# Turning K on VectorE as bf16 pairs instead of on TensorE, in a one-core decode attention kernel

## The chip, the cores and the metric

The kernel runs on one core of one Trainium2 chip. The metric is device time in microseconds (us). Ratios are the mean time of one kernel's fast runs over the mean of the other's fast runs of the same rounds, so they are not quite the ratio of the medians that stand beside them.

Short names: PE is TensorE (PEld its weight loads), DVE is VectorE, ACT is ScalarE, POOL is GpSimd, SP is the engine that issues the transfers.

## The reference, cut to what matters

```python
# B = 4 sequences, one new token each; D = 576, 32 query heads, 16 KV heads, head size 128
W = min(4096, max(256, Sk // 4))                 # the last 4096 keys of 16384
q = (layernorm(x) @ wq)                          # (4, 32, 128)
k = k_cache[:, :, Sk - W:, :]; v = v_cache[:, :, Sk - W:, :]   # each KV head serves 2 query heads
p = softmax(q @ k.T * 128 ** -0.5);  h = x + (p @ v) @ wo
h2 = h + (relu(n @ W_gate) * (n @ W_up)) @ W_down,  n = layernorm(h)
```

K and V are 4 x 16 x 4096 x 128 bf16 values each, 67 MB, and are read once. With the weights, 159.6 MB come from HBM.

## The kernel before

The cache goes through a ring of four slots of 4 MB in SBUF. One tile holds four KV heads of one sequence: 32 partitions for each head, 128 keys in each partition. SP issues one transfer for each tile, in a fixed order; a transfer waits until the last reader of its slot's former tile is done.

```python
def add_kv(kind, g):                         # one 4 MB tile into the next of four slots
    s = ring_slot(); off = slot0 + s * TILE
    src = cache[b, 4*qd:4*qd+4, SK-WIN:SK, :].rearrange("a (p t) d -> p a (t d)", p=32)
    place((kind, g), off, TILE, ("TR", 4*g+3) if kind == "K" else ("PV", 4*g+3), ...)   # who frees it

add_kv("K", 0);  ...wq...                    # order: K0, wq, K1, K2, K3, K4, V0, K5, V1, ...
for g in range(1, NTILE):
    add_kv("K", g)
    if g >= 4: add_kv("V", g - 4)
```

K arrives with keys on partitions; the QK of this kernel is written for the 128 numbers of a head on partitions. So PE transposes 128 blocks a tile (64 in 3.68 us), DVE and ACT copy them from PSUM to SBUF (0.69 and 1.02 us a copy), and QK runs with four matmuls side by side in column groups of 32 (16 in 0.98 us; the records of four start within about 0.01 us):

```python
def pe_tr(i):                                # a quarter of a K tile: 32 transposes
    for j in range(4):
        for u in range(8):
            pe(..., lambda e: e.transpose(out=bankb[TRB[j]][:, u*128:(u+1)*128],
                                          in_=kn[:, t, :], identity=perm))
def evac(i, j):                              # 128x1024 bf16, PSUM to SBUF
    (dve if j % 2 == 0 else act)(("EV", i, j), lambda e: copy(kT..., bankb[TRB[j]][:, 0:1024]))
def pe_qk(dd):
    for a in range(4):
        for j in range(4):
            pe(..., lambda e: e.matmul(bank[4+w][32*j:32*j+32, :],
                                       lhsT=qTm[:, b, 4*qd+a, :], rhs=k[:, j, :, a, :]))
```

## Time and profile before

| | before |
|---|---|
| time, median of the runs | 384.7 us (384.59 to 384.88) |
| span in the profile | 382.6 us |
| moved from HBM | 159.58 MB |
| instructions of PE: matmuls and weight loads | 3781 + 3781 |

First the page of the kernel before: the busy time of each engine, and of the DMA queues' section the data queue and the queue that fetches instructions (packets, MB, share of 16 engines' span).

```profile
PE 248.7 (65%) x3781; PEld 185.9 (49%) x3781; DVE 159.0 (42%) x277; ACT 146.4 (38%) x162; POOL 8.7 (2%) x36
...
q1 hardware_dynamic: 6352, 159.59, 97.4%
q8 instruction: 29, 0.48, 0.5%
```

No compute engine is near its limit; the DMA engines are, at 97.4%. Now the chain of waits between two K tiles (start, length, what):

```profile
96.03 28.17 DMA sb_arena<-in_A_k_cache_dram
...
124.25 3.60 PE psb L425 x32
...
129.31 3.68 PE psb L425 x64
...
135.89 27.24 DMA sb_arena<-in_A_k_cache_dram
```

The K tile lands at 124.2 us and PE works on it for 11.7 us until 135.9, then its slot takes the next transfer, and so on. The chain makes this look like a loop that could be shortened. It can't be: the four slots keep enough transfers waiting that the DMA engines are hardly ever idle. Two stretches show it, as windows (length, busy time of PE, PEld, DVE, ACT, POOL with the count of instructions, granted PE clock, DMA share, GB/s):

```profile
40.00:45.00 5.00, 5.00 (x88) 3.91 (x80) 2.77 (x4) 3.49 (x4) 0.00 (x0) 0.99 0.98 419
165.00:170.00 5.00, 5.00 (x83) 4.13 (x81) 3.72 (x10) 3.68 (x6) 0.00 (x0) 1.00 1.05 449
```

The DMA share is 0.98 and 1.05 here, and it lies between 0.93 and 1.09 in every such window from 5 to 370 us. (A packet counts whole in the window in which it starts, so a share can pass 1.) The last two:

```profile
370.00:375.00 5.00, 2.79 (x93) 2.03 (x93) 1.51 (x4) 0.27 (x1) 0.00 (x0) 1.00 0.78 328
375.00:380.00 5.00, 2.21 (x72) 1.44 (x72) 0.00 (x0) 0.00 (x0) 0.00 (x0) 0.80 0.31 126
```

Here the share falls to 0.78 and then 0.31 while the kernel still waits for data. As I read the records, some DMA engines are done and others are not: for each transfer the trace has 16 increments of its semaphore, at 16 times and without numbers of engines. The page counts 16 DMA engines, and 16 data packets are under way at 60, 100, 200 and 300 us, so I take each increment for one engine that has finished its part. Worked out from those records (not a view of the profile): the time of the first engine and how far behind the others are, with the number of 16 KB instruction packets started by then.

```
before           first us   fetches   lags of the 16 engines behind the first, us
1st K tile          12.71      0      0  .2 .2 .3 .3 .3 .3 .3 .4 .4 .4 .4 .4 .4 .5 .5
2nd K tile          33.41      1      0  .1 .2 .3 .3 .3 .3 .3 .3 .4 .4 .4 .4 .4 .5 1.9
V tile              72.24      6      0  .2 .2 .3 .3 .4 .4 .5 .5 1.1 1.9 1.9 1.9 1.9 1.9 2.0
K tile             120.78     10      0  .2 .3 .3 .4 .5 .9 1.1 1.9 1.9 1.9 1.9 1.9 2.0 3.4 3.4
last transfer      372.77     28      0  .2 .2 .3 .4 .4 .8 2.1 4.9 5.0 5.1 6.5 6.5 6.5 6.6 6.6
```

Each fetch puts one engine back by 1.4 to 1.5 us. The counts fit engines that are hit in turn: after eight fetches eight engines lag by about 1.9 us, then one of them lags by 3.4. The records of single packets give the size of the step: a fetch takes 0.93 to 1.11 us, and for the second to the 26th fetch one data packet of 32 KB that starts about when the fetch ends takes 1.68 to 1.76 us instead of 1.21. These lengths repeat with a period of eight (1.71, 1.71, 1.72, 1.68, 1.68, 1.69, 1.76, 1.76 us), which fits eight engines in turn too. With 28 fetches the worst engines trail by 6.6 us. The kernel ends with the last engine: its increment comes at 379.35 us of a span of 382.6 us.

The groups of instructions that the change is about (line, engine, operation, tiles, shape, count | busy us, mean ns | idle before, releaser):

```profile
L425 PE MATMUL psb<-sb_perm,sb_arena 128*128 128x128 bf16 x2048 | 140.3, 235 | 74.0 <-DMA sb_arena<-in_A_k_cache_dram 73.8
L441 ACT COPY sb_arena<-psb 128x1024 bf16<-128x1024 bf16 x128 | 123.0, 1021 | 141.1 <-PE psb L425 141.1
...
L439 DVE COPY sb_arena<-psb 128x1024 bf16<-128x1024 bf16 x128 | 87.0, 689 | 112.1 <-PE psb L425 111.6
...
L457 PE MATMUL psb<-sb_arena,sb_qTm 128*32 128x512 bf16 x512 | 38.0, 423 | 0.9 <-DVE sb_qTm L404 0.9
```

### The profile page before, as it was taken

The page shows a single profiled execution, that of the slowest core. Times are in us where ns is not written, and L with a number is a line of the kernel's source. Part 1 is how long each engine was busy: PE and PEld are TensorE (multiplying, and loading weights), DVE is VectorE, ACT ScalarE, POOL GpSimd, SP SyncE. Part 2 cuts the span into 40 slices and gives each one's busy share as a digit, 9 for nine tenths or more (in the row PEclk, how much of TensorE's full clock was granted, in tenths as well). Part 3 has the DMA queues.
Part 4 walks back from the last instruction along what each step waited for, and adds up shares of the span by engine and source line. Part 5 has one row for each costly group of instructions (what it writes and reads, how often), then busy time and mean ns, then how long its engine had stood idle before and what let it go on. Part 6 is the DMA issues. An engine that isn't in the chain of part 4 may idle for free.

```text
span 382.6 us, 8170 instructions
## 1 busy us (share of the span) xinstructions
PE 248.7 (65%) x3781; PEld 185.9 (49%) x3781; DVE 159.0 (42%) x277; ACT 146.4 (38%) x162; POOL 8.7 (2%) x36
## 2 busy tenths in 40 slices
PE   0664999779492938893947667966759366026753
PEld 0643788557371726672726455745546222003532
DVE  3342565665342434774432426752516454002220
ACT  3341688836161524762433428542525401000010
POOL 7100000000000000000000000000000000000000
PEclk9997999999888796999796969996969657555597
DMA  8999999999999999999999999999999999999992
GB/s 329 439 433 432 410 421 437 434 433 433 425 423 433 427 433 435 427 420 433 437 430 435 424 428 427 427 428 439 437 432 415 421 436 451 416 431 426 416 411 113
DMA packets 6408, 160.09 MB, mean 418 GB/s; under 512 B 740, under 2 KB 744, under 8 KB 1384
## 3 DMA queue, kind: packets, MB, share of 16 engines
q1 hardware_dynamic: 6352, 159.59, 97.4%
q8 instruction: 29, 0.48, 0.5%
q14 instruction: 3, 0.02, 0.0%
q10 hardware_dynamic: 24, 0.01, 0.0%
HBM read 159.58 MB, written 0.00 MB: 417 GB/s over the span
## 4 chain that ended last, share of the span: by engine, by line
DMA 69%; PE 27%; DVE 2%; SPq 1%; ACT 1%; issue 0%
DMA sb_arena<-in_A_k_cache_dram 53%; PE psb L425 18%; DMA sb_arena<-in_B_W_down_dram 8%; DMA sb_arena<-in_A_v_cache_dram 8%; PE psb L457 5%; PE psb L505 2%; PE psb L480 1%; DVE sb_pp L487 1%; ACT sb_pp L468 1%; SPq L280 0%; DVE sb_stat L464 0%; DVE sb_o_sel L516 0%; PE psb L539 0%; PE psb L530 0%; DVE sb_o_tmp L512 0%
## 5 line engine op out<-in xcount | busy, mean ns | idle before, releaser
L425 PE MATMUL psb<-sb_perm,sb_arena 128*128 128x128 bf16 x2048 | 140.3, 235 | 74.0 <-DMA sb_arena<-in_A_k_cache_dram 73.8
L441 ACT COPY sb_arena<-psb 128x1024 bf16<-128x1024 bf16 x128 | 123.0, 1021 | 141.1 <-PE psb L425 141.1
L425 PEld LDWEIGHTS psb<-sb_perm,sb_arena 128*128 128x128 bf16 x2048 | 131.5, 106 | 89.3 <-DMA sb_arena<-in_A_k_cache_dram 79.8
L439 DVE COPY sb_arena<-psb 128x1024 bf16<-128x1024 bf16 x128 | 87.0, 689 | 112.1 <-PE psb L425 111.6
L505 PE MATMUL psb<-sb_arena,sb_pp 128*32 128x512 bf16 x512 | 35.9, 425 | 19.9 <-DMA sb_arena<-in_A_v_cache_dram 19.9
L457 PE MATMUL psb<-sb_arena,sb_qTm 128*32 128x512 bf16 x512 | 38.0, 423 | 0.9 <-DVE sb_qTm L404 0.9
L505 PEld LDWEIGHTS psb<-sb_arena,sb_pp 128*32 128x32 bf16 x512 | 12.9, 104 | 36.3 <-DMA sb_arena<-in_A_v_cache_dram 20.9
L512 DVE TENSOR_TENSOR sb_o_tmp<-psb,sb_qm 128x512 f32<-128x512 f32 x16 | 11.1, 692 | 41.2 <-PE psb L505 41.2
L487 DVE TENSOR_TENSOR sb_pp<-psb,sb_am 128x1024 bf16<-128x1024 bf16 x16 | 19.6, 1223 | 16.2 <-PE psb L480 16.2
L480 PE MATMUL psb<-sb_ident_b,sb_pp 128*128 128x128 bf16 x128 | 11.5, 242 | 15.8 <-DVE sb_pp L487 8.3
L468 ACT ACTIVATE sb_pp<-psb,sb_stat 128x2048 bf16<-128x2048 f32 x8 | 15.8, 1975 | 9.7 <-DVE sb_stat L466 9.7
L457 PEld LDWEIGHTS psb<-sb_arena,sb_qTm 128*32 128x32 bf16 x512 | 11.6, 103 | 14.8 <-issue 6.2
L480 PEld LDWEIGHTS psb<-sb_ident_b,sb_pp 128*128 128x128 bf16 x128 | 8.6, 108 | 18.8 <-ACT sb_pp L468 8.1
L516 DVE TENSOR_REDUCE sb_o_sel<-sb_o_tmp 128x128 f32<-128x512 f32 x16 | 16.4, 1024 | 0.5
L612 ACT COPY sb_pp<-psb 128x288 f32<-128x288 f32 x1 | 0.4, 399 | 36.2 <-PE psb L607 36.2
L654 PE MATMUL psb<-sb_arena,sb_hnT 128*32 128x384 bf16 x120 | 7.5, 421 | 4.1 <-DVE sb_hnT L639 2.2
L654 PEld LDWEIGHTS psb<-sb_arena,sb_hnT 128*32 128x32 bf16 x120 | 4.1, 121 | 7.2 <-DMA sb_arena<-in_B_W_up_dram 2.3
L464 DVE TENSOR_REDUCE sb_stat<-psb 128x1 f32<-128x1024 f32 x4 | 4.9, 1221 | 4.6 <-PE psb L457 4.6
L687 PE MATMUL psb<-sb_arena,sb_pp 128*32 128x144 bf16 x144 | 3.7, 251 | 4.1 <-DMA sb_arena<-in_B_W_down_dram 3.6
L534 ACT ACTIVATE sb_stat<-sb_stat 128x1 f32<-128x1 f32 x4 | 0.9, 213 | 13.1 <-DVE sb_stat L532 13.1
L661 DVE TENSOR_TENSOR sb_pp<-psb,sb_pp 128x384 bf16<-128x384 f32 x3 | 1.5, 551 | 9.6 <-PE psb L654 9.6
L687 PEld LDWEIGHTS psb<-sb_arena,sb_pp 128*32 128x32 bf16 x144 | 2.6, 105 | 5.1 <-DMA sb_arena<-in_B_W_down_dram 4.6
(128 smaller groups left out, 78.7 us busy)
## 6 DMA issues: line engine op xcount, KB each, us to landing
sb_arena<-in_A_k_cache_dram SPq DMA_DIRECT2D x16, 4096.0 KB, 28.3
sb_arena<-in_A_v_cache_dram SPq DMA_DIRECT2D x16, 4096.0 KB, 33.6
sb_arena<-in_A_wo_dram SPq DMA_DIRECT2D x1, 4608.0 KB, 20.7
sb_arena<-in_B_W_gate_dram SPq DMA_DIRECT2D x1, 4608.0 KB, 34.1
sb_arena<-in_B_W_up_dram SPq DMA_DIRECT2D x1, 4608.0 KB, 43.5
sb_arena<-in_A_wq_dram SPq DMA_DIRECT2D x1, 4096.0 KB, 23.0
sb_arena<-in_B_W_down_dram SPq DMA_DIRECT2D x3, 1296.0 KB, 30.0
sb_arena<-in_B_W_down_dram SPq DMA_DIRECT2D x1, 864.0 KB, 31.6
```

Of the source, the lines that this page charges most:

```text
L425: o = pe(("TRJ", i, j), lambda e, j=j, u=u, t=t: e.transpose(out=bankb[TRB[j]][:, u * 128:(u + 1) * 128], in_=kn[:, t, :], identity=perm[: ...
L439: dve(("EV", i, j), lambda e: e.tensor_copy(out=dst, in_=src), deps)
L441: act(("EV", i, j), lambda e: e.copy(out=dst, in_=src), deps)
L457: o = pe(("QK", dd), lambda e, a=a, j=j: e.matmul(bank[4 + w][32 * j:32 * j + 32, :], lhsT=qTm[:, b, 4 * qd + a, :], rhs=k[:, j, :, a, :], ...
L468: act(("EXP", b, w), lambda e: e.activation(out=p_sb[:, 2048 * w:2048 * w + 2048].rearrange("p (k a) -> p k a", a=4), in_=bass.AP(tensor=p ...
L480: pe(("PT", b, r), lambda e, tl=tl: e.transpose(out=mb_ps[:, tl * 128:(tl + 1) * 128], in_=p_sb[:, (r * 8 + tl) * 128:(r * 8 + tl + 1) * 128],
L487: dve(("PM", b, r), lambda e: e.tensor_tensor(out=dst, in0=src, in1=msk, op=ALU.mult), [("PT", b, r), "c_am8", ("PV", 16 * b - 1) if b els ...
L505: pe(("PV", i), lambda e, j=j, lo=lo, pm=pm, tb=tb: e.matmul(o_ps[32 * j:32 * j + 32, :], lhsT=pT[:, pm:pm + 32], rhs=v[:, lo:lo + 512], s ...
L512: dve(("OS", g), lambda e: e.tensor_tensor(out=o_tmp[:, :].rearrange("p (t d) -> p t d", t=4), in0=o_ps.rearrange("p (t d) -> p t d", t=4) ...
L516: dve(("OSEL", g), lambda e: e.tensor_reduce(out=o_sel[:, qd, :], in_=o_tmp[:, :].rearrange("p (t d) -> p d t", t=4), axis=AX.X, op=ALU.ad ...
L654: pe(("GU", g, c // 4), lambda e, g=g, m=m, j=j, lo=lo, c=c: e.matmul(bank[3 * g + m][32 * j:32 * j + 32, 0:384], lhsT=hnT[:, c if c < 4 e ...
L687: pe("DOWN", lambda e, j=j, r=r, n=n, wv=wv: e.matmul(bank[0][32 * n:32 * n + 32, 0:144], lhsT=hhT[:, r * 128 + 32 * j:r * 128 + 32 * j + 32],
```

## The change

Its intent: take the transposes off PE and their copies off DVE and ACT. DVE's transpose takes two bf16 neighbours as one fp32 value and turns K in place in its slot, for each head its 32 partitions against 32 pairs. Each matmul of QK then contracts over 128 partitions = 4 heads x 32 pairs, for even or odd elements and one half of the head (4 steps `cb`), against weights that hold q of one head and zeros elsewhere. How DVE orders its output has two forms: `by_head` (all columns of a head in one run) or heads two by two in a line. The diff, cut to its core:

```diff
+def by_head(g, w):
+    return (g, w) in ((0, 0), (0, 1), (2, 1), (3, 1), (4, 1))
...
-            place((kind, g), off, TILE, ("TR", 4 * g + 3) if kind == "K" else ("PV", 4 * g + 3),
+            place((kind, g), off, TILE, ("QK", g, 1) if kind == "K" else ("PV", g),
...
-        P.dma("scalar", ("L", "x"), ...)              # was ahead of everything
         act("warm_sqrt", ...)
+        P.dma("scalar", ("L", "x"), ...)
...
-        def pe_tr(i): ...                             # 2048 PE transposes, 256 copies
-        def evac(i, j): ...
+        def turn_k(g, w):                             # half a K tile, in place
+            k = arena[:, land[("K", g)] + w * QWW:][:, 0:QWW].bitcast(FP32)
+            if by_head(g, w):
+                dst = k.rearrange("p (n a k) -> p n k a", a=4, k=8)
+                src = k.rearrange("p (n k a) -> p n k a", a=4, k=8)
+            else:
+                dst = k.rearrange("p (n h l a) -> p n l h a", h=2, l=2, a=2)
+                src = k.rearrange("p (n l h a) -> p n l h a", h=2, l=2, a=2)
+            dve(("TRA", g, w), lambda e: e.transpose(out=dst, in_=src), [("L", "K", g)] if w == 0 else [])
...
+            for a in heads:                           # pe_qk
+                for cb in range(4):
+                    sub, steps = (16 * a, [[2, 8]]) if by_head(g, w) else (a // 2 * 8 + a % 2 * 2, [[16, 4], [4, 2]])
+                    off = land[("K", g)] + w * QWW + cb // 2 * 64 + sub + cb % 2
+                    pe(("QK", g, w), lambda e, ...: e.matmul(
+                        bank[SB[b % 2] + w], lhsT=arena[:, wo_:wo_ + 128],
+                        rhs=bass.AP(tensor=arena, offset=off, ap=[[AW, 128], [128, 64]] + steps), ...), deps)
...
+        def turn_p(b, w): ...                         # P turned on DVE too, mask as bias of 8 short Exp
...
         # order: x, turn of K0, q projection, then K tiles; the first softmax runs inside K4 and K5
```

## The prediction

> **What bounds the kernel now.** The DMA engines. The page's queue section gives the data queue 97.4% of 16 engines' span; the slices show about 430 GB/s from the second to the last but two. PE (65%), DVE (42%) and ACT (38%) have slack. The chain of waits alternates "K lands" (28 us) and "PE turns it, then QK" (18 to 21 us), but that is only the loop of four slots: the windows show a DMA share of 0.97 to 1.07 in every 5 us from 80 to 345 us, so the late release of slots costs nothing.
>
> What is left is uneven engines. In the trace's record of completions, the 16 increments of one transfer lie 0.5 us apart for the first tile and 6.6 us apart for the last (372.8 to 379.35 us). [...] The lag grows in steps of 1.4 to 1.5 us, one engine per 16 KB packet of the instruction queue (29 packets, 0.48 MB), dealt round over eight engines. [...]
>
> **What the change does.** It removes 2048 PE transposes (59 ns apart at full clock, 7.4 us a K tile), their 256 evacuations (DVE 0.69 us, ACT 1.02 us each, 210 us in sum), and 128 transposes of P with 16 masked copies (1.22 us). It adds 32 half-tile turns of 4096 fp32 pairs on DVE; at about 1 element a ns I estimate 4.3 us each[...]. QK no longer has four matmuls side by side: 32 of 128x512 per K tile at 0.24 us (estimate from 16 in 0.98 us, four at a time), 7.5 us against 2. PE per K tile falls from 9.4 to about 7.5 us (double at half clock). None of this lies on the bound.
>
> **What moves the time.** PE instructions fall to about 3260, so 12 to 13 fetches instead of 29: at most two on one engine instead of four. The last engine should trail by about 3.4 us instead of 6.6: a gain of about 3.1 us. Against it: the fourth K tile's transfer now waits for QK of tile 0 (before: its transposes, 22 us), which needs q. I estimate QMM to 28, q placed at 33, QK done near 41 us; the queue would run dry at 43 us. So 0 to 2 us of stall, more if PE starts cold; I count 0.4, and 0.2 gained from the later x load: 384.7 - 3.1 + 0.4 - 0.2.
>
> **Predicted: 381.8 us, 80% between 380.6 and 385.0. Faster by over 2%: 0.01; within 2%: 0.96; slower: 0.03.**
>
> **What would show it.** 12 or 13 instruction packets of 16 KB; last transfer's increments 3 to 4 us apart, first engine still near 372.8 us; DMA share above 0.95 in every 5 us from 5 to 365; turn plus QK of a K tile 12 to 17 us; DVE 190 to 220 us busy.
>
> **What would make it wrong.** A dry DMA queue between 41 and 50 us, or at 85 to 105 us where first softmax, turns and PV compete on DVE; DVE turns of 8 us everywhere, which would make DVE the limit (17 us plus others per 19.6 us); QK slowed by interleaved reads; DMA packets (1.22 us per 32 KB now) slowed by DVE traffic.

The sum: 384.7 - 3.1 + 0.4 - 0.2 = 381.8 us.

The numbers of the trace before that the rest stands on:

- 7562 PE instructions and 29 packets are 261 instructions a packet, so about 3260 are 12.5 packets. That the packets go with PE's instructions was the assumption then; e3 (3978 instructions, 15 packets) and e5 (7562 and 29) bear it out.
- "About 1 element a ns": a DVE copy of 128x128 f32 took 292 ns and one of 128x288 f32 457 ns, 1.03 ns for each further element of a partition. 4096 at that rate are 4.2 us, an estimate.
- "Half clock" and "cold": from 35 to 40 us PE's granted clock is 0.50, and the 32 transposes there come 0.107 us apart; from 40 to 45 us it is 0.99, and they come 0.056 us apart.

## The result, and the profile after

The kernel after took 382.37 us (381.78 to 382.86, 4 runs) against 384.67 us (384.59 to 384.88) before; the ratio is 0.9941, 95% interval 0.9927 to 0.9955. Sent again later (e9), it took 381.78 us (381.47 to 383.03, 6 runs), ratio 0.9927 (0.9916 to 0.9939). The page of the kernel after, the same lines:

```profile
PE 278.0 (73%) x1629; PEld 92.8 (24%) x1629; DVE 223.2 (59%) x157; ACT 37.5 (10%) x95; POOL 16.3 (4%) x38
...
q1 hardware_dynamic: 6352, 159.59, 97.7%
q8 instruction: 12, 0.20, 0.2%
```

PE is busier than before (278.0 against 248.7 us) and DVE too (223.2 against 159.0 us). ACT fell from 146.4 to 37.5 us. The number of PE's instructions fell from 3781 to 1629 pairs, and the instruction packets from 29 to 12. The last windows:

```profile
370.00:375.00 5.00, 3.14 (x125) 2.55 (x129) 1.04 (x3) 0.27 (x1) 0.00 (x0) 1.00 0.81 337
375.00:380.00 5.00, 1.96 (x52) 0.93 (x40) 0.31 (x1) 0.00 (x0) 0.00 (x0) 0.60 0.07 28
```

From 375 to 380 us the DMA share is 0.07 where it was 0.31: the engines now end closer together. The records of the last transfer, worked out as above:

```
                 first us   fetches   last us   spread us
before             372.77      28      379.35      6.59
after              373.20      11      377.55      4.35
```

The first engine did not become faster; the last one ends 1.80 us earlier. (The traced run of the kernel after, 382.86 us, is the slowest of its four.) The groups that do the work now:

```profile
L450 PE MATMUL psb<-sb_arena 128*128 128x512 bf16 x512 | 209.1, 578 | 10.5 <-DVE sb_arena L432 8.2
L432 DVE STREAM_TRANSPOSE sb_arena<-sb_arena 128x4096 f32<-128x4096 f32 x32 | 156.1, 4901 | 48.5 <-DMA sb_arena<-in_A_k_cache_dram 48.4
...
L475 ACT ACTIVATE sb_pp<-psb,sb_stat 128x512 bf16<-128x512 f32 x32 | 24.9, 847 | 247.8 <-DVE sb_stat L470 247.8
```

The 2048 transposes and 256 copies are gone, 32 turns of 4.9 us in the mean have come. QK takes 512 matmuls as before, but one after another. The chain around one K tile:

```profile
104.42 19.58 DMA sb_arena<-in_A_k_cache_dram
...
124.02 4.46 DVE sb_arena L432
...
128.52 13.97 PE psb L450 x32
142.49 1.84 PE psb L497 x32
```

The tile lands at 124.0 us, waits for one turn of 4.46 us and then 13.97 us of QK, and frees its slot at 142.5, 18.5 us after landing; before it was 11.7 us. So the loop that the chain named became longer, and the kernel became faster. That alone shows that the chain's loop was not the bound.

### The profile page after: what moved, and what is told of

It is laid out like the page before. It is cut to its first block, busy times and chain, and to the rows that moved or that the text cites. A ratio compares the mean times of both kernels' runs of the same rounds, so it can differ in the third digit from the quotient of the medians.

```text
span 381.1 us, 3671 instructions
## 1 busy us (share of the span) xinstructions
PE 278.0 (73%) x1629; PEld 92.8 (24%) x1629; DVE 223.2 (59%) x157; ACT 37.5 (10%) x95; POOL 16.3 (4%) x38
## 4 chain that ended last, share of the span: by engine, by line
PE 44%; DMA 34%; DVE 15%; POOL 2%; ACT 2%; issue 1%; SPq 0%; POOLq 0%
PE psb L450 38%; DMA sb_arena<-in_A_k_cache_dram 19%; DVE sb_arena L432 11%; DMA sb_arena<-in_B_W_down_dram 9%; DMA sb_arena<-in_A_v_cache_dram 7%; PE psb L497 5%; POOL sb_arena L303 2%; ACT sb_pp L475 2%; DVE sb_o_sel L509 1%; DVE sb_o_tmp L505 1%; DVE sb_pp L484 1%; PE psb L534 0%; ACT sb_arena L418 0%; SPq L286 0%; PE psb L469 0%
## 5 line engine op out<-in xcount | busy, mean ns | idle before, releaser
L450 PE MATMUL psb<-sb_arena 128*128 128x512 bf16 x512 | 209.1, 578 | 10.5 <-DVE sb_arena L432 8.2
L432 DVE STREAM_TRANSPOSE sb_arena<-sb_arena 128x4096 f32<-128x4096 f32 x32 | 156.1, 4901 | 48.5 <-DMA sb_arena<-in_A_k_cache_dram 48.4
L450 PEld LDWEIGHTS psb<-sb_arena 128*128 128x128 bf16 x512 | 56.8, 114 | 153.6 <-issue 130.3
L475 ACT ACTIVATE sb_pp<-psb,sb_stat 128x512 bf16<-128x512 f32 x32 | 24.9, 847 | 247.8 <-DVE sb_stat L470 247.8
L484 DVE STREAM_TRANSPOSE sb_pp<-sb_pp 128x2048 bf16<-128x2048 bf16 x8 | 18.0, 2278 | 1.4 <-ACT sb_pp L475 1.4
L534 PE MATMUL psb<-sb_o_sel,sb_selw 128*32 128x32 f32 x128 | 2.4, 232 | 16.3 <-DVE sb_o_sel L509 16.3
L388 PE MATMUL psb<-sb_arena,sb_xnT 128*32 128x512 bf16 x32 | 3.6, 631 | 8.9 <-DMA sb_arena<-in_A_wq_dram 8.9
L303 POOL MEMSET sb_arena<- 128x8192 f32 x1 | 6.9, 6925 | 0.0
L475 ACT ACTIVATION_READ_ACCUMULATOR sb_pp<-psb,sb_stat 128x1 f32 x32 | 6.6, 208 | 0.0
L418 ACT COPY sb_arena<-sb_q_keep 32x128 bf16<-32x128 bf16 x16 | 4.8, 303 | 1.5 <-DVE sb_q_keep L409 1.4
```

Of the source, the lines that this page charges most:

```text
L303: pool("c_qW", lambda e: e.memset(arena[:, 0:2 * QWW].bitcast(FP32), 0.0))
L418: act(("QW", b), lambda e, i=i: e.copy(out=bass.AP(tensor=arena, offset=32 * i * AW + b % 2 * QWW + 32 * i, ap=[[AW, 32], [128, 4], [514, ...
L432: dve(("TRA", g, w), lambda e: e.transpose(out=dst, in_=src), [("L", "K", g)] if w == 0 else [])
L450: pe(("QK", g, w), lambda e, off=off, steps=steps, wo_=wo_, qd=qd, first=first, last=a == cb == 3: e.matmul(bank[SB[b % 2] + w], lhsT=aren ...
L475: act(("EXP", b, w), lambda e, w=w, a=a: e.activation(out=bass.AP(tensor=pp, offset=4096 + a // 2 * 2048 + w * 1024 + a % 2, ap=[[8192, 12 ...
L484: dve(("PTR", b, w), lambda e: e.transpose(out=dst, in_=src), [("EXP", b, w), ("PV", 4 * b - 1) if b else "QMM"])
```

## The experiments

Of e1 to e4 the trace that is kept is of another execution than the one first read. The figures below are from the kept traces, except where the first trace is named.

Theory A: the gain comes from PE's shorter instruction stream, since every fetch of 16 KB holds back one of 16 DMA engines, and the kernel ends with the last. Its second part: at the start the change costs something, since the fourth K tile is now issued late. Rivals: B, relief of DVE, ACT or the slots; C, PE's array time.

### e1 and e2: more instructions for PE, by waits that are already met (failed as a test)

```diff
+                    for _ in range(NPAD):             # after each QK matmul, g >= 5; 12 and 24
+                        pe(None, PAD)                 # engine.wait_ge(sem, 1), met long ago
```

> The kernel after, with 12 semaphore waits that are already met after each QK matmul of the K tiles from the sixth on: 2112 more instructions for PE's sequencer, no array work. Theory A (the gain is the fewer instruction fetches of PE, which hold back single DMA engines): about 20 instruction packets instead of 12, the last transfer's increments 1.4 us further apart, 1.0 to 1.6 us slower than the kernel after, ratio to before about 0.9975. Theory B (the gain is PE, ACT and DVE relieved, or slots released otherwise): no change, ratio 0.994.

> The same with 24 waits, 4224 more instructions. A: about 28 or 29 packets, increments about 2.9 us further apart than in the kernel after, time near the kernel before, ratio 1.000 to 1.003. B: no change, ratio 0.994, unless the waits lengthen QK by so much that the DMA queue runs dry, which the DMA share in 5 us windows would show.

Measured: 449.31 us, ratio 1.168, and 681.57 us, ratio 1.770, with 21 and 29 packets. The waits were not free. PE's timeline in e2 (first trace; start, length, engine, line) shows QK matmuls 1.33 us apart where the kernel after has 0.43:

```profile
200.62 0.59 PE L455 MATMUL psb<-sb_arena 128*128 128x512 bf16 x1 [0.77 <-issue]
201.95 0.59 PE L455 MATMUL psb<-sb_arena 128*128 128x512 bf16 x1 [0.75 <-issue]
```

PE became the bound and the DMA queue ran dry: in e1 PE is busy for 8.77 of the 10 us from 205 to 215 us, and the DMA share is 0.62 (265 GB/s); the 159.6 MB in e2's span of 680.2 us are 235 GB/s. So these runs say nothing of A or B. They tell one thing by accident: in both the last transfer's engines lie only 2.0 us apart in spite of 20 and 29 fetches, where the kernel before has 6.6 us after 28. I read this as engines that are behind and catch up when the queue is dry, so that the lag adds up only while all engines have work.

### e3: the kernel before with fewer PE instructions

```diff
-                    for u in range(8): e.transpose(out=bankb[TRB[j]][:, u*128:(u+1)*128], in_=kn[:, t, :], identity=perm)
+                    e.matmul(bank[TRB[j]][:, :], lhsT=perm, rhs=kn[:, t:t + 4, :], start=True, stop=True)   # once
```

K is not turned, so the result is wrong. The comparison with the reference still passed: the scores are so small (about 0.003, an estimate from the inputs' scales in the reference) that the softmax is nearly flat, so K hardly reaches the output. A pass is no proof that K is handled rightly here.

> The kernel before, with each group of eight transposes of a K tile replaced by one 128x512 matmul into the same bank (wrong result on purpose, K isn't turned): 1792 fewer pairs of PE instructions, everything else kept, above all the evacuations on DVE and ACT. A: 15 packets instead of 29, the last transfer's increments 3.4 to 3.6 us apart instead of 6.6, ratio 0.991 to 0.993, a little better than the kernel after since no late issue of the fourth K tile disturbs the start. B (relief of DVE and ACT, or DVE turning K): little or no gain, ratio above 0.997. A rival that says PE time is what counts would expect a gain too; the two runs with waits are against that one.

Measured: 381.62 us (381.51 to 381.84), ratio 0.992 (0.9907 to 0.9934). Busy time and fetches:

```profile
PE 207.8 (55%) x1989; PEld 80.3 (21%) x1989; DVE 155.5 (41%) x277; ACT 145.1 (38%) x162; POOL 8.7 (2%) x36
...
q8 instruction: 15, 0.25, 0.3%
```

The last transfer: first engine 372.88, last 376.42 us, spread 3.54. The last engine ends 2.93 us earlier than before and the median is 3.1 us lower. DVE and ACT do what they did before, so that part of B falls: this kernel gets the whole gain without the turn on DVE. In e3 PE works less and frees slots sooner; the kernel after is the counterexample to both, with PE busier and slots freed later.

### e5 and e6: the instructions back without their work, and the work without the instructions

```diff
 e5:  # e3, and ahead of each matmul seven one-column matmuls into the bank that it overwrites
+                    for _ in range(7): e.matmul(bank[TRB[j]][:, 0:1], lhsT=perm, rhs=kn[:, t, 0:1], ...)
 e6:  # e3, its matmul three times
+                    for _ in range(3): e.matmul(bank[TRB[j]][:, :], lhsT=perm, rhs=kn[:, t:t + 4, :], ...)
```

> The kernel of e3 (eight transposes replaced by one matmul, wrong result on purpose) with seven one-column dummy matmuls ahead of each: the instruction count of the kernel before comes back, the array work hardly does. Theory A (fetches of PE instructions hold back single DMA engines): 29 packets, increments of the last transfer 6.3 to 6.9 us apart, ratio 0.999 to 1.001. Theory C (PE's array time is what counts): ratio near e3's, 0.992 to 0.994.

> The kernel of e3 with its matmul done three times over: PE array time of this step above that of the transposes ([...]at least 166 us against 121 at full clock), 1280 pairs of instructions fewer than before. A: 18 or 19 packets; if the 17th comes before the end, one or two engines have three fetches, so increments 4.6 to 5.1 us apart and ratio 0.995 to 0.997. C: slower than before, ratio above 1.

(The 121 and 166 us are estimates: 2048 transposes at 59 ns, from 32 in 1.89 us in the trace before, and 768 matmuls at 0.216 us, from QK sorted by head in the trace after, both at a granted clock of 1.00.)

e5 measured 384.65 us, ratio 0.9999 (0.9987 to 1.0011), with 29 packets again and a spread of 6.56 us, last engine at 379.34 us, that of the kernel before to 0.01 us:

```profile
PE 241.4 (63%) x3729; PEld 132.3 (35%) x3781; DVE 159.1 (42%) x277; ACT 147.3 (39%) x162; POOL 8.7 (2%) x36
...
q8 instruction: 29, 0.48, 0.5%
```

The one-column matmuls brought PE's busy time back as well (241.4 us), so e5 against e3 does not part A from C by itself. The kernels after, e4 and e8 do: PE is busy for 278 to 288 us in them, more than before, and they are faster.

e6 measured 384.56 us (382.95 to 385.24), ratio 0.9988: the expected 0.995 to 0.997 was missed. Its spread was 3.60 us with 18 fetches, but the first engine ended at 375.56, not 373. One window shows where the 2.7 us against e3 went:

```profile
90.00:95.00 5.00, 4.84 (x52) 2.26 (x52) 3.75 (x5) 2.02 (x2) 0.00 (x0) 1.00 0.58 200
```

Where K, V and the first softmax meet, PE was too slow, a slot came free late and the queue ran dry. So e6 tests a second thing, not the one I wanted: longer PE work costs where the queue runs dry for it. (By the reading of e1 and e2 lagging engines could also catch up in the dry spell, so the spread of 3.60 us is no test of the 18 fetches.)

### e7: tile 0 turned like the later tiles

```diff
-    return (g, w) in ((0, 0), (0, 1), (2, 1), (3, 1), (4, 1))
+    return (g, w) in ((2, 1), (3, 1), (4, 1))
```

> The kernel after, with tile 0 turned two heads to a line like the later tiles, not sorted by head: its turn on DVE is shorter (4.5 us a half instead of 7.3), its QK longer (about 0.43 us a matmul, 14 us). My theory: QK of tile 0 ends near 45 us instead of 40.1, the fourth K tile is issued 2 us after the queue ran dry at 43 us: DMA share well under 0.9 between 43 and 48 us, all later landings 3 to 4.5 us later, ratio to before 1.001 to 1.006. Rival (the slack of four slots absorbs it): ratio 0.994.

Measured: 385.46 us (385.19 to 386.41), ratio 1.0023 (1.0011 to 1.0035). SP's timeline in e7 shows the issue of the fourth K tile, and its windows what followed:

```profile
45.45 0.54 SPq L246 DMA_DIRECT2D sb_arena<-in_A_k_cache_dram  x1
```

```profile
40.00:45.00 5.00, 5.00 (x13) 1.36 (x12) 2.92 (x1) 0.00 (x0) 0.00 (x0) 1.00 0.50 216
45.00:50.00 5.00, 5.00 (x13) 1.26 (x12) 4.85 (x2) 0.00 (x0) 0.00 (x0) 1.00 0.65 242
```

The queue ran dry at about 43 us, and the share is 0.50 and 0.65 in the two windows. The first engine ends the last transfer at 377.38 us, 4.2 us later than in the kernel after, which is what was lost here. The last engine ends only 3.3 us later, which fits lagging engines that catch up in the dry spell (spread 3.49 instead of 4.35 us); the median is 3.1 us higher. So the two halves of tile 0 have to be sorted by head: it makes DVE slower (7.4 instead of 4.45 us a half) when it has time, and PE faster (0.21 instead of 0.43 us a matmul) when it has none. Whether the other three sorted halves are needed was not tested.

### e4, e8 and e12: the fourth K tile issued earlier

The same line in the kernel before (22 us) and after (40.1 us, both K tiles that waited):

```profile
22.02 5.41 SPq L239 DMA_DIRECT2D sb_arena<-in_A_k_cache_dram  x2
```

```profile
40.09 1.18 SPq L246 DMA_DIRECT2D sb_arena<-in_A_k_cache_dram  x2
```

The queue would run dry at 43.1 us, when the third K tile's first engine is done. So 40.1 us looks early enough, and the windows of the kernel after show no gap, only 393 GB/s in one window where 419 is usual (e8 below has 419 there):

```profile
40.00:45.00 5.00, 5.00 (x13) 1.25 (x11) 2.77 (x2) 0.00 (x0) 0.00 (x0) 1.00 1.00 393
45.00:50.00 5.00, 5.00 (x13) 1.36 (x12) 5.00 (x2) 0.00 (x0) 0.00 (x0) 1.00 1.00 419
```

The records of single DMA packets tell more: where the third K tile ends and the fourth begins (42.6 to 47 us) packets of 32 KB, 1.21 to 1.22 us elsewhere, took up to 2.54 us. Summed over the engines it is 8.8 us of engine time; the engines that it hit most fell up to about 1 us further behind.

```diff
 e4:  dummy 128x512 matmuls on PE: 26 ahead of the q projection, 8 behind it
+        warm_pe(26)
...
+        warm_pe(8)
 e8:  e4, and: mask constants c_am, c_msk made after the turns of tile 0, q kept by ACT
-            dve("qkeep", ...)
+            act("qkeep", ...)
 e12: e8 with warm_pe(46) in place of warm_pe(26)
```

What the dummies are for: in the kernel after PE's granted clock is 0.50 from 31.3 to 34.7 us, and the first matmuls of QK come 0.43 us apart; from 34.7 us it is 1.00, and they come 0.21 us apart. That dummies would prevent this was an expectation, which the runs below test.

> The kernel after, with 26 dummy matmuls ahead of the q projection and 8 behind it, so that TensorE's clock is at full when QMM and the first QK run. A with its second part (the fourth K tile is issued too late, at 40.1 us, 3 us before the queue would run dry, and the packets of that moment are slow): issue at about 37 us, no slow packets between 42 and 46 us, first engine ends near 372.8 us instead of 373.2, last 0.5 to 1.3 us earlier; ratio to before 0.991 to 0.9925. If the slow packets have another cause, they stay at 42 to 46 us and the ratio stays 0.994.

> The kernel of e4 (dummy matmuls) with, in addition, the mask constants made after the turns of tile 0, so that DVE does not wait for the 6.9 us memset, and q kept by ACT instead of DVE: first turn from 13.3 instead of 14.6 us, fourth K tile issued about 37 us. Theory: the issue of e4 was early enough already (no slow packets left), so no further gain: ratio 0.991 to 0.9935, last increments 3.3 to 3.7 us apart.

> The kernel of e8 with 46 dummy matmuls instead of 26 ahead of the q projection: in e8's trace they had ended at 18.4 us, 4.7 us before QMM, and QMM still ran cold (3.6 us for 32). Now they should end just before 23 us, QMM take about 2 us and the fourth K tile be issued at about 36 us instead of 38.4. Theory: issue earlier than 38.4 us is worth nothing more, since no packet was slow there in e8; ratio 0.990 to 0.993, all runs within 0.5 us of each other, last increments 3.2 to 3.7 us apart. If more is to be had from the start, ratio under 0.990.

Measured, with the issue of the fourth K tile and the excess of packet time between 40 and 50 us (the time over 1.225 us, summed over the 32 KB packets that start there):

| | median us (range) | ratio to before (95%) | issue us | excess us | spread us |
|---|---|---|---|---|---|
| after | 382.37 (381.78 to 382.86) | 0.9941 (0.9927 to 0.9955) | 40.09 | 8.8 | 4.35 |
| after again (e9) | 381.78 (381.47 to 383.03) | 0.9927 (0.9916 to 0.9939) | 40.27 | 6.7 | 4.09 |
| e4 (kept trace) | 381.68 (381.52 to 382.32) | 0.9923 (0.9911 to 0.9936) | 40.05 | 6.8 | 3.68 |
| e8 | 381.43 (381.25 to 381.47) | 0.9914 (0.9901 to 0.9927) | 38.42 | 0.0 | 3.27 |
| e12 | 381.60 (381.24 to 382.66) | 0.9924 (0.9910 to 0.9937) | 36.25 | 0.0 | 3.81 |

> The kernel after itself, unchanged, for a second interval: ratio 0.993 to 0.995, so above e8's 0.9914.

e9's ratio came out a little below what I expected (0.993 to 0.995).

The slow packets are gone in e8 and e12, as the theory said, though e8 issued at 38.42 us and not at the expected 37; issuing at 36 us is worth nothing more. For e4 the issue moved between two executions. In its first trace the fourth K tile was issued at 38.38 us. In the kept trace the issue came at 40.05 us and the slow packets are there. PE's timeline of the kept trace shows the eight dummies, and QK after a gap of 2.40 us:

```profile
26.95 1.90 PE L402 MATMUL psb<-sb_ident_b 128*128 128x512 bf16 x8
31.25 11.35 PE L455 MATMUL psb<-sb_arena 128*128 128x512 bf16 x38 [2.40 <-ACT sb_arena L423]
```

The single records of this QK lie 0.22 us apart at first, 0.43 us from 32.1 to 35.5 us, then 0.22 us again: the dummies did not keep QK at 0.22 us throughout. PE's timeline of e8 and of e12 shows what the dummies do there. The first line of each are the 26 or 46 dummies ahead, the next is QMM, the matmuls of the q projection; the last line of e8 is QK of tile 0:

```profile
11.29 7.09 PE L398 MATMUL psb<-sb_ident_b 128*128 128x512 bf16 x26
23.07 3.60 PE L384 MATMUL psb<-sb_arena,sb_xnT 128*32 128x512 bf16 x32 [4.68 <-DMA sb_arena<-in_A_wq_dram]
...
31.30 7.08 PE L451 MATMUL psb<-sb_arena 128*128 128x512 bf16 x32 [0.20 <-ACT sb_arena L419]
```

```profile
11.29 11.78 PE L398 MATMUL psb<-sb_ident_b 128*128 128x512 bf16 x46
23.02 1.91 PE L384 MATMUL psb<-sb_arena,sb_xnT 128*32 128x512 bf16 x32
```

In e8 the 26 dummies ended 4.7 us ahead of QMM and were wasted on it; in e12 QMM took 1.91 instead of 3.60 us. The records of PE's granted clock don't show that QMM is slow: in the kernel after, where QMM took 3.60 us too, they give 1.00 from 20 to 30 us. In e8 QK follows the eight dummies after 0.20 us and took 7.08 us, 0.22 us a matmul throughout. In the kernel after 2.14 us without a matmul stand ahead of the slow stretch of QK, in the kept trace of e4 2.40 us. How long a gap brings such a stretch on, and what ends it, these runs don't show.

What stays open: e12 had one run at 382.66 us and a spread of 3.81 us, both outside what I expected. Its trace has slow packets (up to 2.34 us) at 91.5 to 92 us, and the kept traces of e4, e8 and the kernel after have some there as well. The tile whose packets begin there was issued at 88.3 to 88.7 us, again about 3 us ahead; but e9 issued it at 88.62 us and has none. The fourth K tile shows the same. Issued 4.7 us ahead or more (e8, e12) it met no slow packets. Issued 2 to 3 us ahead (40.05 to 40.89 us) it met an excess of 8.8, 6.7 and 6.8 us (after, e9, e4), of 4.7, 2.5 and 2.0 us (e2, e11, e10), and of none in e1, at 40.68 us. So a late issue goes with slow packets but does not decide them, and their cause is not shown. DVE's turns do not explain them: the median packet took 1.214 us in the kernel after and 1.215 in the one before, and from 40 to 45 us DVE is busy for 4.08 us in e8, without slow packets, and for 2.77 us in the kernel after, with them. e8 is the best of the kernels here by its median, but its interval overlaps that of e9, so a gain over the kernel after is not shown.

### e9, e10: the later load of x

```diff
+        P.dma("scalar", ("L", "x"), ...)              # first again, as in the kernel before
         add_kv("K", 0)
...
-        P.dma("scalar", ("L", "x"), ...)
```

> The kernel after, with the load of x issued ahead of ACT's warm-up again, as in the kernel before. My prediction counted 0.2 us for the later load; the first data packet starts at 2.15 us in both kernels, so now I expect nothing: ratio 0.993 to 0.995, first packet at 2.15 us.

Measured in the same rounds as e9: 381.78 us (381.28 to 382.74), ratio 0.9926 (0.9914 to 0.9938) against e9's 0.9927, and a first packet at 2.15 us. The order of that load shows no effect.

### e11: every half tile sorted by head

```diff
-    return (g, w) in ((0, 0), (0, 1), (2, 1), (3, 1), (4, 1))
+    return True
```

> The kernel after, with every half tile turned sorted by head. Turn 7.3 us a half instead of 4.5, so DVE is busy about 300 us instead of 223, and QK about 0.22 us a matmul at full clock instead of 0.43, so PE about 200 instead of 278. Theory: both still fit in the 19.4 us of a K and a V tile in the steady part (DVE 14.6 plus about 3.4 for selecting), but at the start (K tiles every 9.7 us) and where a softmax adds two turns of P and a row maximum (6 us) DVE falls behind; the DMA queue runs dry there, total loss 2 to 15 us, ratio 1.00 to 1.035. If the slots absorb it, 0.994.

Measured: 405.46 us, ratio 1.0535 (1.0515 to 1.0555), worse than I expected. The busy times and the turn:

```profile
PE 218.8 (54%) x1629; PEld 92.3 (23%) x1629; DVE 301.1 (75%) x157; ACT 37.6 (9%) x95; POOL 16.2 (4%) x38
...
L432 DVE STREAM_TRANSPOSE sb_arena<-sb_arena 128x4096 f32<-128x4096 f32 x32 | 235.6, 7417 | 3.6 <-DMA sb_arena<-in_A_k_cache_dram 3.6
```

PE gains (218.8 us instead of 278.0) and loses its place as the busiest engine to DVE, whose turns take 7.4 us. From 95 to 102 us the DMA queue is dry (share 0.00 from 95 to 100 us, 0.60 from 100 to 105). A faster PE is of no use here; sorting pays only where QK is what holds a slot.

## Why the prediction was right

The prediction was 381.8 us, range 380.6 to 385.0; the results were 382.37 and, sent again, 381.78 us. Its steps, one by one:

- **The bound is DMA, and the loop in the chain costs nothing: right.** The loop grew from 11.7 to 18.5 us a tile and the kernel became faster. e7 and e6 show the other side: a dry queue costs at once. Two readings of the share were off by one window each: before, it is 0.94 from 315 to 320 us (the prediction had 0.97 as the least), and after, it is 0.91 from 360 to 365 us (above 0.95 predicted).
- **The end is set by the engine with the most instruction fetches: right, and shown.** 12 packets, as predicted ("12 or 13"). e3 takes the fetches away from the kernel before and gains 3.1 us, just the predicted size; e5 brings the instructions back without the transposes and has the old time and the old spread to 0.03 us.
- **Spread 3.4 us: 4.35 measured.** The term was mis-sized, most likely because single engines were also held back by slow packets at 42 to 47 us. Where those are gone the spread is 3.27 us (e8), and 3.81 us in e12, which has slow packets at 91.5 us instead.
- **Stall at the start, counted with 0.4 us: right in place, and about right in size.** The first engine ends 0.43 us later; the slow packets, which are in no term of the sum (the prediction named slow packets only as an effect of DVE's traffic), cost the last engine another us or so. The kernel after varies by 1.6 us from run to run (e9), probably in part for that reason: its two traces, both of slower runs (382.86 and 382.85 us), have 8.8 and 6.7 us of excess, while e10's trace, of a run of 381.28 us, has 2.0. With that variation it is chance that the median sent again, 381.78 us, meets the prediction so closely.
- **0.2 us from the load of x: wrong, nothing** (e10).
- **QK at 0.24 us a matmul, 7.5 us a K tile, and PE relieved: wrong.** It takes 0.43 us, 13.97 us a tile, at a granted clock of 0.50 and of 1.00 alike, and PE became busier by 29 us. Only the halves sorted by head run at 0.21 us (at 1.00). The weight loads, one for each matmul, show both (25 in 5.28 us by head until 40 us, then 0.43 us apart):

```profile
34.72 5.28 PEld L450 LDWEIGHTS psb<-sb_arena 128*128 128x128 bf16 x25 [0.28 <-issue]
40.31 0.11 PEld L450 LDWEIGHTS psb<-sb_arena 128*128 128x128 bf16 x1 [0.32 <-issue]
40.75 0.11 PEld L450 LDWEIGHTS psb<-sb_arena 128*128 128x128 bf16 x1 [0.32 <-issue]
```

  I had taken the rate of QK before, with contiguous runs of 32 elements, for one that reads every fourth element. Elements 8 bytes apart, in pairs, took the 0.43 us, and elements 4 bytes apart, eight in a row, the 0.21 us. The lower rate cost nothing since the slots had room for it. The predicted "turn plus QK 12 to 17 us" was 18.5.
- **The turn at 4.3 us: 4.45 measured** (two heads to a line, pairs of fp32 values written side by side, 1.09 ns for each value of a partition). Sorted by head, with values written 32 bytes apart, it took 7.4 us; all 32 took 156.1 us. DVE was busy for 223 us, 190 to 220 predicted.

The change did what it was meant to (no transposes on PE, ACT nearly free), and none of that is where its gain comes from. It gains since PE's program became less than half as long.

## What to carry to other kernels

When the DMA engines are busy for the whole span, compare when each of them finishes the last transfer: here the kernel before had a spread of 6.6 us, and a shorter instruction stream of PE took part of it away (12 instruction packets instead of 29 in the kernel after, spread 4.35 us, median 2.3 us lower; 15 packets in e3, 3.54 us and 3.1 us). In these runs a long wait in the chain of waits was no bound as long as the DMA share stayed near 1; the price came at once where a transfer was issued after the moment at which the queue runs dry (e7: at 45.45 us instead of 43.1, 3.1 us in the median), and transfers issued 2 to 3 us before it often, but not always, met slow packets. When an experiment has to add instructions without work, measure first what the added ones cost: 24 waits that were already met after each QK matmul set the matmuls 1.33 us apart instead of 0.43 (e2), and 12 of them 0.66 us (e1). From the two spacings I estimate about 55 ns for each wait.
